# Eight clamps of decoded weight pieces move from VectorE to GpSimd

## The chip, the cores and the metric

The kernel runs on one core of one Trainium2 chip, as one program. The metric is the device time of that core in microseconds. Five engines work side by side, each through its own queue and in the order of that queue: TensorE (PE: matmuls into the accumulator memory PSUM), VectorE (DVE), ScalarE (ACT), GpSimd (POOL) and SyncE (SP: it issues transfers). They meet at semaphores only.

## The reference, cut to what matters

Eight batches of an attention over 32 memory slots per head, whose output goes through a two-layer network with a squared ReLU. q, k, v and phi are float32; the two weight matrices of the network are float64.

```python
a = softmax(phi, over the sequence)          # per memory slot
k_m, v_m = einsum(a, k), einsum(a, v)        # 32 x 64 per head
attn = softmax(q @ k_m.T / 8) @ v_m          # per head
x = attn, laid out as 4608 tokens x 512
h = maximum(x @ w_in, 0)                     # w_in 512 x 2048, float64
out = (h * h @ w_out).astype(float32)        # w_out 2048 x 512, float64
```

## The kernel before

**What is computed where.** TensorE never multiplies `attn` itself: each batch's values are folded into `w_in` first (`u`, by `make_u` or `late_u`), and `u` is multiplied with the attention weights `a` (`ffn1`, L672), squared, and multiplied with `w_out` (`ffn2`, L693 and L701). Batches 0 and 1 run as 64 steps in the order of `runs`; each step is one `ffn1` of 128 rows of `d_ff` and, two steps later, its `ffn2`. In the first 16 steps batch 0 takes an unsplit float32 copy of `u` and `a`; later ones take each factor as a high and a low part. Batches 2 to 7 follow in another scheme (`late_*`), from some 200 us on.

**The weights.** [...] Each matrix is loaded as raw 8-byte words (`fetch_w_in`, `fetch_w_out`) and `decode` turns a piece of 128 x 512 or 128 x 1024 words into float32. There are 17 pieces: `("in", n, q0)` for `w_in`, of which the first two, (0,0) and (0,1), are halves of 128 x 512; `("out", k)` for `w_out`, k from 0 to 7. I write in(0,0) or out 1 for them.

**The steps of one decode, with the lines of the profile:**

1. L575, ScalarE: the upper word of each number, read as float32, loses its sign and goes to the tile `tmp` (two buffers). For in(2,0) VectorE does it instead (L581).
2. L578, ScalarE: the lower word, scaled, goes to the tile `low` (one buffer).
3. L582, VectorE: the magnitude in `tmp` is clamped between `LEAST` and `MOST`, in place: two comparisons in one instruction.
4. L584, VectorE: shift by three bits and mask, in place.
5. L587, VectorE: the sign and the top exponent bit of the upper word are put in; reads the raw piece and `tmp`.
6. L594, the `adder` given by the caller: `tmp` + `low` is the float32 weight. It goes to `w_sb` (for `w_in`) or to `wp` or `tmp` (for `w_out`). It is GpSimd for in(0,0) and in(0,1), VectorE for the other six pieces of the change.

`decode` stops at two places (`yield`), ahead of step 3 and ahead of step 6, and the caller goes on with other work there.

**What sets the order.** It is written out by hand. The string `order` interleaves the first work: `d0`, `d1` and `d2` are the decodes of in(0,0), in(0,1) and in(1,0), `o0` that of out 0, `a0` and `a1` are the two attention halves of batch 0, `v0` and `u0` the two halves of the first `u`. After it, the table `plan` says at which half step each later piece goes on: out 1 at 3, 6 and 8, in(3,0) at 8, 9 and 11, out 2 from 20 on, out 3 from 31 on. Each engine then works off its queue in that order. So L582 of a piece stands at a fixed place between other VectorE instructions, for example between L482 and L584 for in(1,0).

**Other lines that are named below.** L201 and L209 are TensorE's transpose and broadcast for the softmax of `phi` of batch 1 (VectorE's L187 to L190 ahead of them, L204 between them, L223 behind). L434 is `by_heads`, also for the attention scores. In `attend`, VectorE's L460 or L462 transposes the scores, L466 and L470 subtract their maximum, ScalarE's L472 is the exponential, VectorE's L479 to L482 normalise and L487 or L492 transposes back; L494 and L495 (or L502 and L504 in `split_a`) split the result into `a_hi` (ScalarE) and `a_lo` (GpSimd or VectorE). L550 makes `u_lo` on VectorE. L685 makes `g_lo` on GpSimd from step 16 on. L112 fills rows of a tile of keys with zeros, on GpSimd.

Of the kernel before, what the change touches and what calls it, by code (L numbers as in the profile page):

```python
# [14 lines left out]
ALU = mybir.AluOpType  # L15
# [5 lines left out]
LEAST = 2.0 ** -15  # L21
MOST = 2.0 ** 17 - 2.0 ** 13 - 2.0 ** -7
# [3 lines left out]
def attn_moe_kernel(ctx: ExitStack, tc: tile.TileContext, qT, kv, phi, w_in, w_out, outT):  # L26
# [12 lines left out]
    nc = tc.nc  # L39
# [93 lines left out]
    def new_ps(main=False):  # L133

        if starting and not main:
            n = len(starting) - 1
            starting.append(True)
            return [ps_acc.tile([P, 512], F32, name=f"acc{2 * (n % 2) + i}") for i in range(2)]
        assert not ps_user, (now, ps_user)
        ps_user.append(list(now))  # L140
        return ps_m.tile([P, 2, 512], F32, name="ps_m")

    def done_ps(ps):
        if not isinstance(ps, list):
            ps_user.pop()

    def bank(ps, i):
        return ps[i] if isinstance(ps, list) else ps[:, i]
# [279 lines left out]
    def by_heads(out, mem, x, rhs):  # L428

        for pr in range(NPAIR):  # L430
            for half in range(2):
                hs = slice(D * half, D * (half + 1))
                y = rhs[pr // NQ][hs, pr % NQ]
                nc.tensor.matmul(  # L434
                    bank(out, half)[M * pr:M * (pr + 1), :y.shape[-1]], mem[hs, x, pr], y, start=True, stop=True
                )

    def half_heads(out, mem, x, rhs, half):

        hs = slice(D * half, D * (half + 1))  # L440
        for pr in range(NPAIR):
            y = rhs[pr // NQ][hs, pr % NQ]
            nc.tensor.matmul(out[M * pr:M * (pr + 1), :y.shape[-1]], mem[hs, x, pr], y, start=True, stop=True)  # L443
# [117 lines left out]

    on_vector = {("in", 2, 0)}

    def decode(raw, new_out, adder, key):

        n = raw.shape[1] * raw.shape[2]

        def word(w, dtype):
            return raw.bitcast(dtype).rearrange("p j (n w) -> p (j n) w", w=2)[:, :, w]


        c = work.tile([P, 2 * DM], I32, name="tmp", bufs=2)[:, :n]
        size = c.bitcast(F32)
        if key not in on_vector:
            nc.scalar.activation(size, word(1, F32), AF.Abs)  # L575

        r = work.tile([P, 2 * DM], I32, name="low", bufs=1)[:, :n]
        nc.scalar.activation(r, word(0, U32), AF.Copy, scale=2.0 ** -29)  # L578
        yield
        if key in on_vector:  # L580
            nc.vector.tensor_scalar(out=c, in0=word(1, I32), scalar1=0x7FFFFFFF, scalar2=None, op0=ALU.bitwise_and)  # L581
        nc.vector.tensor_scalar(out=size, in0=size, scalar1=LEAST, scalar2=MOST, op0=ALU.max, op1=ALU.min)  # L582

        nc.vector.tensor_scalar(  # L584
            out=c, in0=c, scalar1=3, scalar2=0x3FFFFFF8, op0=ALU.logical_shift_left, op1=ALU.bitwise_and
        )
        nc.vector.scalar_tensor_tensor(  # L587
            out=c, in0=word(1, I32), scalar=-0x40000000, in1=c, op0=ALU.bitwise_and, op1=ALU.bitwise_or
        )
        yield  # L590
        out = c if new_out is None else new_out().bitcast(I32)
        if len(out.shape) > 2:
            c, r = (x.rearrange("p (a n) -> p a n", a=out.shape[1]) for x in (c, r))
        adder.tensor_tensor(out=out, in0=c, in1=r, op=ALU.add)  # L594
        return out.bitcast(F32)
# [19 lines left out]
    def decode_in(n, q0, q1, adder=nc.gpsimd):  # L615

        def new_out():
            if n // 2 not in w_in_at:
                w_in_at[n // 2] = new_w()
            return w_in_at[n // 2][:, 2 * q0:2 * q1, n % 2 * HC:n % 2 * HC + HC]  # L620

        assert all(("in", n, qd) in fetched for qd in range(q0, q1))
        yield from decode(raws["in", n][:, q0:q1], new_out, adder, ("in", n, q0))
        ready.update(("in", n, qd) for qd in range(q0, q1))
        if all(("in", n ^ i, x) in ready for i in range(2) for x in range(NQ)):
            if starting:
                kept.append(n // 2)
                return
            yield
            keep_w(n // 2)  # L630

    def decode_out(k, adder=nc.gpsimd, whole=False):

        def new_out():
            w = room(k, [P, 2, DM], F32)
            wo[2 * k:2 * k + 2] = [w[:, 0], w[:, 1]]
            return w

        assert all(("out", k, i) in fetched for i in range(2))
        w = yield from decode(raws.pop(("out", k)), new_out if whole else None, adder, ("out", k))  # L640
        if not whole:
            yield
            yield from split(k, w.rearrange("p (i x) -> p i x", i=2))
        ready.update(("out", 2 * k + i) for i in range(2))
# [61 lines left out]
    banks = {}  # L706
    current = [-1]

    held = {}

    def hold(name, who):
        assert name not in held, (name, who, held)
        held[name] = who

    def drop(name, who):
        assert held.pop(name) == who
# [227 lines left out]
    def late_u(b, n):  # L944

        assert ("mem", b) in ready
        drop("w", (b, n))
        for i in range(2):
            hold(f"raw{i}", (b, 2 * n + i))
        w = late_rooms["w"]  # L950
        if "raw" not in late_rooms:
            late_rooms["raw"] = work.tile([P, 2, 4, P], F32, name="low", bufs=1)
            late_rooms["e"] = {}
        raw = late_rooms["raw"]
        first = b == JOIN and not n
        x = (state[b]["mem"], 1, [w[:, :NQ], w[:, NQ:]])
        if first:
            ps = new_ps(True)
            by_heads(ps, *x)
        else:  # L960
            assert banks["open"]
            hold("side", ("u", b, n))
            ps = [banks["z" if "m" in held else "m"], banks["h"][(current[0] + 1) % 2]]
            if beside:
                half_heads(*beside.pop(0))
                sc = banks["m"]
                nc.scalar.copy(sc[:, T3:T3 + 1], sc[:, T3 - 1:T3])
                half_heads(ps[1], *x, 1)
                half_heads(ps[0], *x, 0)
                half_heads(*beside.pop(0))  # L970
            else:
                by_heads(ps, *x)
        yield
        for qd in (1, 0):
            (nc.scalar.copy if late_on[f"raw{qd}"] >> n & 1 else nc.vector.tensor_copy)(raw[:, :, 2 * (1 - qd):2 * (1 - qd) + 2], bank(ps, qd).rearrange("p (a i n) -> p a i n", a=2, i=2))
        if first:
            done_ps(ps)
        else:
            drop("side", ("u", b, n))
        ready.update(("raw", b, 2 * n + i) for i in range(2))  # L980

    def late_split(b, p):
# [441 lines left out]
    for places, fn, *args in plan:  # L1424
# [6 lines left out]

    late_plan = [
        ((32, 33), late_u, 0, 3),
        ((0, 1), late_u, 0, 1),
        ((33, 33, 33, 35, 38), late_split, 0, 6),
        ((1, 3, 8, 9, 13), late_split, 0, 2),
        ((18, 19, 21, 22, 24), late_split, 0, 4),
        ((3, 8, 8, 11, 16), late_split, 0, 3),
        ((20,), late_stream, 0, 3),
        ((36, 37, 40, 41, 48), late_split, 0, 7),  # L1440
        ((16, 16), late_u, 0, 2),
        ((7,), late_stream, 0, 2),
        ((21, 22, 27, 27, 32), late_split, 0, 5),
# [92 lines left out]
    for k, step in enumerate(steps):  # L1536
        i, b, t, f = step
# [4 lines left out]
        n = f * P // FC  # L1542
        u, a = state[b]["u"][n][0], state[b]["a32" if alone else "a"][t]
# [50 lines left out]
    z = banks["z"]  # L1594
# [56 lines left out]
    n = (B - JOIN) * REST  # L1651
# [79 lines left out]
```

## Time and profile before

| | us |
|---|---|
| median of three runs | 700.79 (700.62 to 700.91) |
| the profiled execution, first to last instruction (its span) | 698.8 |
| TensorE busy | 683.1 (98%) |
| VectorE busy | 502.3 (72%) |
| ScalarE busy | 437.6 (63%) |
| GpSimd busy | 315.9 (45%) |

The profile shows one execution. Its span runs from the first to the last instruction; the time of a run is taken from outside and holds 1.99 us more (700.79 less 698.8). TensorE's granted clock is 1.00 of full speed, its level of 2.4 GHz, in every stretch of the table of stretches.

Rows of a timeline read: start, duration, engine, line, operation, result <- operands, shape, count, and in brackets the idle time of the engine before it with what ended it. Rows of one engine can overlap by some 0.08 us, because an instruction may start while the last one empties. In the chain of waits each piece begins where the one before it ended; "issue" there is time in which nothing was waited for.

### The profile page before, as it was taken

How to read it: one execution, taken by the hardware profiler on the slowest of the kernel's cores; microseconds unless marked ns; L12 is line 12 of the kernel's file. 1: busy time of each engine (PE TensorE's matmuls, PEld its weight loads, DVE VectorE, ACT ScalarE, POOL GpSimd, SP SyncE). 2: the span in 40 equal slices, each digit the busy share in tenths (PEclk: the TensorE clock that was granted, in tenths of full speed). 3: DMA queues.
4: the chain of work that ended last, by engine and by line, in shares of the span. 5: the costliest groups of instructions: out<-in, count | busy, mean ns of one | idle time of the engine just before them, and what ended most of it. 6: DMA issues, size and time to landing. Idle time of an engine off the chain costs nothing.

```text
span 698.8 us, 14172 instructions
## 1 busy us (share of the span) xinstructions
PE 683.1 (98%) x5104; PEld 574.2 (82%) x5104; DVE 502.3 (72%) x1167; ACT 437.6 (63%) x1204; POOL 315.9 (45%) x481
## 2 busy tenths in 40 slices
PE   8789999999999999999999999999999999999997
PEld 4367889999998888888888887888878888888897
DVE  3988868655888977888878977797787775555432
ACT  2566788886456675567566665667566666665531
POOL 1200253443348465645665564745474566444200
PEclk9999999999999999999999999999999999999999
DMA  9996353509423922184136613291206110400002
GB/s 289 350 376 242 118 175 83 186 2 264 139 62 129 289 75 76 46 244 139 42 121 188 175 61 122 85 275 63 83 1 212 69 51 19 150 32 1 28 33 47
DMA packets 67847, 89.86 MB, mean 129 GB/s; under 512 B 6848, under 2 KB 56064, under 8 KB 64192
## 3 DMA queue, kind: packets, MB, share of 16 engines
q1 hardware_dynamic: 65888, 87.41, 38.7%
q10 hardware_dynamic: 1888, 1.54, 0.7%
q8 instruction: 40, 0.66, 0.4%
q14 instruction: 31, 0.25, 0.1%
HBM read 75.30 MB, written 13.63 MB: 127 GB/s over the span
## 4 chain that ended last, share of the span: by engine, by line
PE 87%; DVE 9%; ACT 1%; issue 1%; POOL 1%; POOLq 0%; DVEq 0%; ACTq 0%
PE acc L1092 35%; PE h L1116 10%; PE acc L701 9%; PE z L1116 7%; PE h L672 6%; PE acc L693 4%; PE h L1681 2%; DVE mem L400 1%; PE ps_m L434 1%; PE z L443 1%; DVE u_lo L996 1%; PE m L1681 1%; PE z L1681 1%; PE m L322 1%; PE m L443 1%; PE h L154 1%
## 5 line engine op out<-in xcount | busy, mean ns | idle before, releaser
L1092 PE MATMUL acc<-u_hi,wp 128*128 128x512 f32 x576 | 153.9, 396 | 0.0
L1092 PE MATMUL acc<-u_lo,wp 128*128 128x512 f32 x576 | 140.0, 392 | 0.0
L1092 PEld LDWEIGHTS acc<-u_hi,wp 128*128 128x128 f32 x576 | 101.2, 188 | 26.0 <-issue 11.0
L1092 PEld LDWEIGHTS acc<-u_lo,wp 128*128 128x128 f32 x576 | 105.5, 188 | 20.4
L996 POOL TENSOR_TENSOR u_lo<-low,u_hi 128x256 fp32r<-128x256 f32 (+1 forms) x106 | 68.9, 661 | 47.8 <-ACT u_hi L995 44.9
L685 POOL TENSOR_TENSOR g_lo<-g,g_hi 128x288 fp32r<-128x288 f32 x48 | 44.4, 925 | 80.6 <-ACT g_hi L683 55.7
L1140 POOL TENSOR_TENSOR u_hi<-g_lo,u_hi 128x288 fp32r<-128x288 f32 (+1 forms) x70 | 53.2, 761 | 43.5 <-ACT g_lo L1137 21.1
L701 PE MATMUL acc<-g_hi,wp 128*128 128x288 f32 x360 | 59.0, 298 | 0.2 <-DVE o L1173 0.2
L995 ACT CAST u_hi<-low 128x256 fp32r<-128x256 f32 (+1 forms) x160 | 52.7, 347 | 8.4 <-POOL low L1007 7.2
L1132 DVE CUSTOM_DVE_ANT_0 g_hi<-h,g_hi 128x288 f32<-128x288 f32 x95 | 42.6, 449 | 19.8 <-ACT g_hi L1163 19.2
L1163 ACT COPY g_hi<-z 128x288 f32<-128x288 f32 x72 | 28.7, 399 | 44.2 <-PE z L1116 43.1
L701 PEld LDWEIGHTS acc<-g_hi,wp 128*128 128x128 f32 x360 | 51.2, 188 | 4.9 <-ACT r L674 1.7
L1135 ACT ACTIVATE u_hi<-g_hi 128x224 fp32r<-128x224 f32 x95 | 39.0, 411 | 22.1 <-DVE g_hi L1132 22.0
L1158 POOL TENSOR_TENSOR u_lo<-g_lo,u_lo 128x288 fp32r<-128x288 f32 x30 | 25.1, 838 | 55.2 <-DVE g_lo L1157 49.2
L674 ACT ACTIVATE r<-h 128x288 f32<-128x288 f32 x64 | 26.0, 406 | 31.6 <-PE h L672 31.5
L1157 DVE TENSOR_TENSOR g_lo<-h,g 128x288 f32<-128x288 f32 x48 | 21.6, 450 | 25.0 <-ACT g L1153 25.0
L693 PE MATMUL acc<-g_hi,wp 128*128 128x288 f32 x128 | 33.8, 410 | 1.6 <-DVE wp L594 1.6
L1116 PE MATMUL z<-a_hi,u_hi 128*128 128x288 f32 x120 | 35.3, 294 | 0.0
L1116 PE MATMUL h<-w_sb,u_hi 128*128 128x288 f32 x120 | 34.3, 298 | 0.8 <-DVE g_hi L1132 0.8
L1116 PE MATMUL h<-a_lo,u_hi 128*128 128x288 f32 x120 | 34.6, 295 | 0.0
L701 PE MATMUL acc<-g_lo,wp 128*128 128x288 f32 x180 | 34.6, 295 | 0.0
L1135 ACT ACTIVATE u_lo<-g 128x224 fp32r<-128x224 f32 x48 | 18.8, 391 | 23.6 <-DVE g L1132 23.5
(366 smaller groups left out, 1789.5 us busy)
## 6 DMA issues: line engine op xcount, KB each, us to landing
w_sb<-w_f SPq DMA_DIRECT2D x24, 1024.0 KB, 5.2
wp<-in_w_in SPq DMA_DIRECT2D x16, 512.0 KB, 8.2
wp<-in_w_out SPq DMA_DIRECT2D x16, 512.0 KB, 7.4
kvb<-in_kv SPq DMA_DIRECT2D x28, 256.0 KB, 7.1
tmp<-in_kv SPq DMA_DIRECT2D x24, 256.0 KB, 6.1
q_sb<-in_q SPq DMA_DIRECT2D x15, 384.0 KB, 5.7
w_f<-w_sb SPq DMA_DIRECT2D x4, 1024.0 KB, 6.2
e_sb<-in_phi SPq DMA_DIRECT2D x7, 512.0 KB, 7.1
```

Source lines behind the costliest of these rows:

```text
L672: nc.tensor.matmul(h[:, :T], u[:, qd, fs], x[:, qd], start=(i == 0), stop=(i == len(todo) - 1))
L685: nc.gpsimd.tensor_tensor(out=g_lo, in0=g, in1=g_hi.bitcast(F32), op=ALU.subtract)
L693: nc.tensor.matmul(acc[e][:, :T], wo[f][:, e * P:(e + 1) * P], g_hi, start=first, stop=last)
L701: nc.tensor.matmul(acc[e][:, :T], wo[f][:, w, e * P:(e + 1) * P], x, start=first and x is g_hi and w == 0, stop=last and x is g_lo,)
L995: nc.scalar.copy(hi[:, k], x)
L996: by(name, p).tensor_tensor(out=lo[:, k], in0=x, in1=hi[:, k].bitcast(F32), op=ALU.subtract)
L1092: nc.tensor.matmul(late_accs[e], wo[f][:, w, e * P:(e + 1) * P], x, start=f == 0 and first, stop=f == NFT - 1 and last,)
L1116: nc.tensor.matmul(out[:, :T], u[:, lhs], a, start=first and not n, stop=n == 2, skip_group_check=not first)
L1132: nc.vector._custom_dve(TENSOR_ADD_SAT, out=x, in0=u[:, :T], in1=x, s0=float("inf"), s1=0.0)
L1135: nc.scalar.square(g_hi, x[:, :n])
L1140: by(f"c{k}", p).tensor_tensor(out=g_lo, in0=g[:, :n], in1=g_hi.bitcast(F32), op=ALU.subtract)
L1163: (nc.vector.tensor_copy if late_on[f"z{k}"] >> pairs[j][1] & 1 else nc.scalar.copy)(x, banks["z"][:, :T])
```

## The change

The diff, whole. `on_pool` names eight pieces, and for these step 3 goes to GpSimd. The second part makes `late_u` record that it holds the bank `m` while it uses it; it chooses the same bank as before.

```diff
     on_vector = {("in", 2, 0)}
 
+    on_pool = {("in", 0, 0), ("in", 0, 1), ("in", 1, 0), ("out", 0), ("out", 1), ("in", 3, 0), ("out", 2), ("out", 3)}
+
     def decode(raw, new_out, adder, key):
...
-        nc.vector.tensor_scalar(out=size, in0=size, scalar1=LEAST, scalar2=MOST, op0=ALU.max, op1=ALU.min)
+        (nc.gpsimd if key in on_pool else nc.vector).tensor_scalar(
+            out=size, in0=size, scalar1=LEAST, scalar2=MOST, op0=ALU.max, op1=ALU.min
+        )
...
-            ps = [banks["z" if "m" in held else "m"], banks["h"][(current[0] + 1) % 2]]
+            own = "m" not in held
+            if own:
+                hold("m", ("u", b, n))
+            ps = [banks["m" if own else "z"], banks["h"][(current[0] + 1) % 2]]
...
             drop("side", ("u", b, n))
+            if own:
+                drop("m", ("u", b, n))
```

In the changed file all lines behind `on_pool` have higher numbers: L582 becomes L584 there, L584 L588, L587 L591, L594 L598, L685 L689.

GpSimd's queue over the whole start, before. In the names, `tmp_253` is in(0,0), `tmp_270` in(0,1), `tmp_308` in(1,0), `tmp_347` out 0, `tmp_438` out 1, `tmp_568` in(3,0), `tmp_753` out 2 and `tmp_896` out 3; `u_hi4_380` is the tile of keys:

```order
L594 TENSOR_TENSOR w_sb_303<-tmp_253,low_255 128x2x256
L594 TENSOR_TENSOR w_sb_303<-tmp_270,low_272 128x2x256
L112 MEMSET u_hi4_380 64x512
L504 TENSOR_TENSOR a_lo0_414<-a_hi2_344,a_hi0_413 128x576
L495 TENSOR_TENSOR a_lo3_771<-at_772,a_hi3_770 128x576
L504 TENSOR_TENSOR a_lo1_640<-u_lo0_436,a_hi1_639 128x576
```

The same stretch of GpSimd's queue now:

```order
L584 TENSOR_SCALAR tmp_253<-tmp_253 128x512
L598 TENSOR_TENSOR w_sb_303<-tmp_253,low_255 128x2x256
L584 TENSOR_SCALAR tmp_270<-tmp_270 128x512
L598 TENSOR_TENSOR w_sb_303<-tmp_270,low_272 128x2x256
L584 TENSOR_SCALAR tmp_308<-tmp_308 128x1024
L584 TENSOR_SCALAR tmp_347<-tmp_347 128x1024
L112 MEMSET u_hi4_380 64x512
L584 TENSOR_SCALAR tmp_438<-tmp_438 128x1024
L584 TENSOR_SCALAR tmp_568<-tmp_568 128x1024
L504 TENSOR_TENSOR a_lo0_414<-a_hi2_344,a_hi0_413 128x576
L584 TENSOR_SCALAR tmp_753<-tmp_753 128x1024
L495 TENSOR_TENSOR a_lo3_771<-at_772,a_hi3_770 128x576
```

The fill of the keys now stands behind the clamps of in(1,0) and out 0, the subtraction of L504 also behind those of out 1 and in(3,0), and that of L495 also behind that of out 2.

VectorE's queue at in(1,0) and out 0, before (`w_sb_303` is the decoded `w_in`, `wp0_406` the decoded out 0):

```order
L482 TENSOR_TENSOR st_277<-st_277,acc1_279 128x576
L582 TENSOR_SCALAR tmp_308<-tmp_308 128x1024
L584 TENSOR_SCALAR tmp_308<-tmp_308 128x1024
L587 SCALAR_TENSOR_TENSOR tmp_308<-wp5_118,tmp_308 128x1024
L487 STREAM_TRANSPOSE a_hi2_344<-st_277 128x576
L594 ISA w_sb_303<-tmp_308,low_310 128x4x512
L582 TENSOR_SCALAR tmp_347<-tmp_347 128x1024
L584 TENSOR_SCALAR tmp_347<-tmp_347 128x1024
L587 SCALAR_TENSOR_TENSOR tmp_347<-wp0_120,tmp_347 128x1024
L594 ISA wp0_406<-tmp_347,low_349 128x2048
```

And now:

```order
L482 TENSOR_TENSOR st_277<-st_277,acc1_279 128x576
L588 TENSOR_SCALAR tmp_308<-tmp_308 128x1024
L591 SCALAR_TENSOR_TENSOR tmp_308<-wp5_118,tmp_308 128x1024
L487 STREAM_TRANSPOSE a_hi2_344<-st_277 128x576
L598 ISA w_sb_303<-tmp_308,low_310 128x4x512
L588 TENSOR_SCALAR tmp_347<-tmp_347 128x1024
L591 SCALAR_TENSOR_TENSOR tmp_347<-wp0_120,tmp_347 128x1024
L598 ISA wp0_406<-tmp_347,low_349 128x2048
```

The two rows of L582 are gone, nothing else has moved, and each L588 now waits for GpSimd.

## Rows read from the trace of the kernel before

**Rows 1.** By stretches: window, length, busy us of each engine, clock, DMA
```profile
46.00:690.00 644.00, 641.81 (x4654) 549.17 (x4654) 468.49 (x1105) 414.03 (x1165) 308.46 (x460) 1.00 0.36 115
```

**Rows 2.** Chain of waits, first 140 us: start us, us, what
```profile
16.52 0.34 DVE tmp L582
...
20.38 0.35 DVE tmp L582
...
23.95 0.70 DVE tmp L582
...
28.42 0.61 DVE tmp L582
...
36.37 0.41 PE ps_m L201 x2
...
39.69 0.46 PE ps_m L209 x4
...
41.72 0.61 DVE tmp L582
```

**Rows 3.** GpSimd by form: count, busy us, mean ns, idle before
```profile
L1001 POOL TENSOR_TENSOR g_hi<-low 128x128 f32<-128x128 f32 x18 | 8.3, 460 | 0.0
...
L594 POOL TENSOR_TENSOR w_sb<-tmp,low 128x1024 int32<-128x1024 int32 x1 | 2.4, 2414 | 0.0
...
L112 POOL MEMSET u_hi<- 64x512 f32 x2 | 1.0, 520 | 0.1
...
masks.py:199 POOL TENSOR_SCALAR_AFFINE_SELECT ident<-ident 128x128 f32<-128x128 f32 x1 | 0.3, 292 | 0.1
```

**Rows 4.** Timeline, 87 to 90 us: start us, us, engine, line, [idle before]
```profile
87.59 1.60 DVE L594 CUSTOM_DVE_ANT_0 tmp<-tmp,low 128x2048 uint16<-128x2048 uint16 x1
...
88.36 1.49 POOL L685 TENSOR_TENSOR g_lo<-g,g_hi 128x288 fp32r<-128x288 f32 x1 [0.25 <-ACT g_hi L683]
...
89.37 1.04 DVE L582 TENSOR_SCALAR tmp<-tmp 128x1024 f32<-128x1024 f32 x1 [0.17 <-ACT tmp L575]
```

**Rows 5.** Timeline of three engines, 69 to 75 us
```profile
69.08 0.76 DVE L482 TENSOR_TENSOR st<-st,sm 128x576 f32<-128x576 f32 x1
...
72.50 2.00 POOL L495 TENSOR_TENSOR a_lo<-at,a_hi 128x576 fp32r<-128x576 f32 x1 [38.85 <-ACT a_hi L494]
...
74.54 0.30 PEld L672 LDWEIGHTS h<-a_lo,u_hi 128*128 128x128 f32 x2 [0.16 <-POOL a_lo L495]
```

**Rows 6.** ScalarE's timeline: absolute values of five pieces
```profile
15.26 0.67 ACT L575 ACTIVATE tmp<-wp 128x512 f32<-128x512 f32 x1 [4.53 <-DMA wp<-in_w_in]
...
22.06 1.15 ACT L575 ACTIVATE tmp<-wp 128x1024 f32<-128x1024 f32 x1 [0.74 <-DMA wp<-in_w_in]
...
26.25 1.19 ACT L575 ACTIVATE tmp<-wp 128x1024 f32<-128x1024 f32 x1
...
35.34 1.12 ACT L575 ACTIVATE tmp<-wp 128x1024 f32<-128x1024 f32 x1
...
67.65 1.14 ACT L575 ACTIVATE tmp<-wp 128x1024 f32<-128x1024 f32 x1
```

**Rows 7.** GpSimd's timeline: the addition of the first piece
```profile
18.22 1.27 POOL L594 TENSOR_TENSOR w_sb<-tmp,low 128x512 int32<-128x512 int32 x1 [14.69 <-DVE tmp L587]
```

**Rows 8.** VectorE's timeline, 27 to 39 us
```profile
27.24 1.18 DVE L594 CUSTOM_DVE_ANT_0 w_sb<-tmp,low 128x2048 uint16<-128x2048 uint16 x1
...
37.44 0.76 DVE L482 TENSOR_TENSOR st<-st,sm 128x576 f32<-128x576 f32 x1
...
38.93 0.39 DVE L204 TENSOR_REDUCE nmx<-ps_m 128x2 f32<-128x256 f32 x1
```

**Rows 9.** TensorE's timeline at 45.7 us
```profile
45.73 2.21 PE L693 MATMUL acc<-g_hi,wp 128*128 128x288 f32 x8 [0.41 <-DVE wp L594]
```

**Rows 10.** VectorE's timeline: two places where its queue stands idle
```profile
52.04 0.78 DVE L462 STREAM_TRANSPOSE st<-ps_m 128x576 f32<-128x576 f32 x1 [1.24 <-PE ps_m L434]
...
95.42 1.22 DVE L550 TENSOR_TENSOR u_lo<-ps_m,u_hi 128x1024 fp32r<-128x1024 f32 x1 [1.89 <-ACT u_hi L548]
```

## The prediction

> **What bounds the kernel now.** I read the busy time of each engine by stretches first: from 46 to 690 us TensorE is busy for nearly all of the 644 us [rows 1]. So whatever happens beside it there is free as long as it is not late. Then I read the chain of waits over the first 140 us, because the eight clamps all stand early. Before TensorE's L201 at 36.37 us, and again between its L209, which ends at 40.15, and 45.7 us, the chain runs mostly on VectorE, and the clamp of L582 is on it five times: 0.34, 0.35, 0.70, 0.61 and 0.61 us [rows 2]. These belong to the pieces in(0,0), in(0,1), in(1,0), out 0 and out 1. The other three moved clamps, in(3,0), out 2 and out 3, are not on the chain. So the most that the change could take off is 2.6 us (the five added up), and only if GpSimd hands each clamped piece over before VectorE would have wanted it.
>
> That the change does not do what it says can be excluded from the order of the instructions: eight clamps leave VectorE and eight stand on GpSimd, and no other row of any engine differs. The `hold` and `drop` lines in `late_u` only record who uses a bank and leave no instruction behind.
>
> **The price of a clamp on GpSimd.** The trace has no such instruction there. GpSimd's two-input additions take 0.46 us for 128 elements a partition and 2.41 us for 1024, so 2.18 ns an element and 0.17 to 0.18 us fixed. The one instruction there that reads one tile and writes one, the mask of 128 elements, takes 0.29 us: with the same fixed part, 0.12 us for 128 elements, or 0.94 ns an element. The fill, which reads nothing, takes 0.52 us for 512 [rows 3]. The clamp reads one tile and writes one, like the mask, so I take the mask's rate: 0.66 us for 512 elements and 1.14 us for 1024. The ends are the fill's rate (0.52 us, and twice its 0.34 above the fixed part, 0.86 us, for 1024) and the two-input rate (1.30 and 2.41 us).
>
> The Trainium skill (GPSIMD Engine Reference, Engine selection) says that one-input work on GpSimd is roughly at line rate and that elementwise work otherwise belongs on VectorE, where it is about twice as fast. By its clock of 1.2 GHz, 1024 elements would be about 0.85 us plus the fixed part, an estimate that would make the sum some 0.2 us smaller than mine.
>
> **One port between the two engines.** At 87.59 us VectorE's addition of L594 (two tiles read) starts and ends at 89.19; GpSimd's subtraction that starts at 88.36 takes 1.49 us and ends 0.66 us after VectorE's end. The next VectorE clamp starts at 89.37, while that subtraction runs, and takes 1.04 us: it ends 0.56 us after GpSimd's end, where an undisturbed one takes 0.70 (at 23.95) [rows 2, 4]. So the one that is second stands until the first is done, and then needs about 0.13 us less than alone.
>
> The Trainium skill (SBUF — State Buffer, Who interferes with whom) says the same: the pair of ports is locked for a whole instruction, against VectorE instructions with two SBUF inputs or in a two-port mode. The trace agrees, with the 1.04 us above.
>
> **The change part by part.** A hand-over between GpSimd and another engine takes 0.04 us where TensorE waits for it (74.50 to 74.54 [rows 5]); I take 0.05 each way.
>
> in(0,0): the absolute value is done at 15.26 + 0.67 = 15.93 us [rows 6]. The clamp runs from 15.98 to 16.64 on GpSimd and L584 starts at 16.69; before, it started at 16.88 (16.52 + 0.34 + 0.02). VectorE itself is free at 16.52. Gain 0.19.
>
> in(0,1): GpSimd must first finish the addition of in(0,0), at 19.49 [rows 7], now 19.30. The clamp ends at 19.96. VectorE reaches this place at 20.38 - 0.19 = 20.19, so nothing waits. Gain 0.19 + 0.37 = 0.56.
>
> in(1,0): the absolute value waited for its weights from memory and ends at 22.06 + 1.15 = 23.21 whatever VectorE does [rows 6]. The clamp runs to 24.40, L584 starts at 24.45, and before at 24.67 (23.95 + 0.70 + 0.02). Of the 0.56 us gained, 0.22 are left: VectorE now waits where it had worked.
>
> out 0: here the port decides. VectorE's addition for in(1,0) started at 27.24 [rows 8] and now starts at 27.02, and it ends at 28.20. The absolute value of out 0 ended at 27.44 (26.25 + 1.19 [rows 6]); it stands on ScalarE behind work that moves with in(0,0), so it ends at 27.25 at best. GpSimd is second, stands until 28.20, needs 1.01 us more, and L584 starts at 29.26. Before, it started at 29.05. So up to here the change loses 0.21 us. From here the chain stays on VectorE until TensorE's L201 at 36.37 us [rows 2], which waits for it, so the loss goes through. GpSimd's fill for the keys is queued behind this clamp and no longer before it; the keys are multiplied only after L209 [rows 2], more than 10 us later, so I cost it at nothing. If it got the port just ahead of L584, that would cost up to its 0.52 us [rows 3].
>
> out 1: the absolute value ends at 36.46 [rows 6], the clamp at 37.65, more than 3 us before VectorE needs it, at 41.72 [rows 2]. It collides with L482, which reads two tiles and starts at 37.44 [rows 8]: 0.21 us, less the 0.13. VectorE's L204 ends at 38.93 + 0.39 = 39.32 and TensorE's L209 starts at 39.69 behind other TensorE work [rows 2, 8], so 0.3 us are hidden there. Then 0.71 us are gone from VectorE ahead of the addition for out 1, whose result TensorE awaited for 0.41 us at 45.73 [rows 9]. Behind that wait comes TensorE's own preceding work. Gain 0.41.
>
> in(3,0) and out 3: the VectorE queue behind them waits anyway, 1.24 us for TensorE at 52.04 and 1.89 us for ScalarE at 95.42 [rows 10]. The subtraction of L504, now queued on GpSimd behind the clamps of out 1 and in(3,0), slips from 32 us to 46 us; its result belongs to a later use of the split, since the first 16 steps take the unsplit copy. Nothing for all of these; if the cover were gone, each would cost one clamp, 1.1 us.
>
> out 2: the clamp starts at 67.65 + 1.14 + 0.05 = 68.84 on GpSimd, 0.24 us before VectorE's L482 at 69.08, which reads two tiles. L482 stands until 69.98 and ends at 70.61 instead of 69.84, 0.77 late; the removed clamp gives back 0.71 (as at 23.95). The subtraction of L495 on GpSimd comes out of this queue, and TensorE waits for it with no slack at 74.54 [rows 5]. Loss 0.06.
>
> **Sum.** 698.8 + 0.21 - 0.41 + 0.06 = 698.7 us of span. The median of the runs, 700.79, is 1.99 us above the profiled span; I add that to every sum here. Forecast 700.7.
>
> **Rivals.** *GpSimd's clamp is slow* (slower). The place is out 0 and then out 2, through the port. At 1.78 us for 1024, halfway to the two-input rate, in(1,0) is 0.42 late, the clamp of out 0 comes in ahead of VectorE's addition (27.62 against 27.66), and that stands until 29.40: L584 is 1.40 late. At out 1, L482 stands for 0.85 us, which eats the gain of 0.41. At out 2 another 0.70 is lost. Together 2.1, so 702.9; at the full two-input rate about 4, so 704.8. Between -0.1 at 1.14 us and 2.1 at 1.78 us, it passes 1.4 us of loss at about 1.58 us. For it speaks that this is two comparisons in one instruction, which no row shows; against it the mask's rate.
>
> *No lock for one-input work* (a little faster). If GpSimd ran beside VectorE, out 0 would be clamped at 28.44 and L584 would gain 0.56 instead of losing 0.21; with the 0.41, 699.8. Against it speaks that the VectorE instruction that stood at 89.37 was a one-input one.
>
> With the fill's rate and the lock, L584 of out 0 gains 0.35, in all some 0.7: 700.1. That is the near end of the forecast, not another case.
>
> **How the numbers follow.** Forecast 0.60, the slow clamp 0.24, no lock 0.11, and 0.05 for something unseen on either side. The measurement tells about 0.2%, 1.4 us, from no change. The forecast and the unlocked case lie within that; the slow clamp lies above it from 1.58 us on, most of its weight. So faster 0.06, same 0.71, slower 0.23. The range goes from 699.7 (no lock) to 703.0 (the slow clamp's 702.9); the full two-input rate and a gain beyond 1.1 us are left out.
>
> **What would show it.** A GpSimd clamp of 1024 elements at 1.0 to 1.3 us where nothing runs beside it; VectorE idle before L588 (the old L584) for in(1,0), about 1 us, with GpSimd as the one that ends it; GpSimd's clamp of out 0 stretched to 2 us across VectorE's addition; no TensorE wait at out 1. I am wrong if that clamp takes 1.6 us or more alone, if out 0 is clamped before 28.2 us, or if TensorE's gap at 74.5 us has grown by more than 0.3 us.

## The result: 708.1 us, ratio 1.0097, and the profile after

The changed kernel takes 708.1 us (median, 706.48 to 709.29) against 700.79 us: a ratio of 1.0097, 95% interval 1.0084 to 1.011. That is slower by some 6.8 us, where the prediction expected 700.7 and allowed up to 703.0. The span of the profiled execution is 705.4 us, against 698.8.

The first view is the line L584 by itself (duration in ns, least/median/most; first and last start; forms). It answers to [rows 3].

```profile
L584 POOL TENSOR_SCALAR tmp<-tmp x8: 1916/3622/4161, 15.7 to 89.1; 128x1024 f32<-128x1024 f32 x6, 128x512 f32<-128x512 f32 x2
...
who waited for it (us, times):
  DVE tmp L588: 12.0, 6
```

A clamp takes 1.92 us for 512 elements and 3.62 for 1024, where VectorE took 0.41 and 0.69. VectorE waited for it six times, 12.0 us in all. The chain of waits (start us, us, what) shows where that lies on the path; it answers to [rows 2], in which the clamp stood five times with 0.34 to 0.70 us and always on VectorE.

```profile
15.73 1.93 POOL tmp L584
...
20.26 1.89 POOL tmp L584
...
24.72 3.63 POOL tmp L584
...
89.13 3.88 POOL tmp L584
...
93.04 1.30 DVE tmp L588
...
97.47 1.17 ACT low L580
```

The pieces in(0,0), in(0,1) and in(1,0) now put GpSimd itself on the chain. So does out 3 at 89.13, which was not on the chain at all before. In VectorE's timeline (start us, us, what, idle before and what ended it) the waits of the start are these:

```profile
17.68 0.43 DVE L588 TENSOR_SCALAR tmp<-tmp 128x512 int32<-128x512 int32 x1 [1.49 <-POOL tmp L584]
...
22.17 0.43 DVE L588 TENSOR_SCALAR tmp<-tmp 128x512 int32<-128x512 int32 x1 [1.00 <-POOL tmp L584]
...
28.37 0.69 DVE L588 TENSOR_SCALAR tmp<-tmp 128x1024 int32<-128x1024 int32 x1 [2.98 <-POOL tmp L584]
29.10 1.94 DVE L591 SCALAR_TENSOR_TENSOR tmp<-wp,tmp 128x1024 int32<-128x1024 int32 x1
...
32.76 0.92 DVE L588 TENSOR_SCALAR tmp<-tmp 128x1024 int32<-128x1024 int32 x1
```

The sum of the start: 1.49 + 1.00 + 2.98 = 5.47 us of waiting; L591 at 29.10 needs 1.94 us instead of 1.23, because GpSimd's clamp of out 0 gets going beside it, 0.71 more; and L588 at 32.76 needs 0.92 instead of 0.69, because GpSimd's fill L112 (32.61, 0.52 us) came in ahead of it, 0.23 more. That makes 6.41. The four clamps that left VectorE gave back 0.41 + 0.42 + 0.69 + 0.68 = 2.20, and this execution reached this place 0.32 us earlier (L412 at 15.78 instead of 16.10). 6.41 - 2.20 - 0.32 = 3.89, and TensorE's L201 is 3.93 us later, at 40.30 instead of 36.37 [rows 2].

TensorE's timeline gives the lateness at six places. First after, then the rows of before that [rows 2, 9] don't hold:

```profile
40.30 0.41 PE L201 MATMUL ps_m<-ident,phi_mx 128*128 128x128 f32 x2
...
49.69 2.21 PE L697 MATMUL acc<-g_hi,wp 128*128 128x288 f32 x8
...
65.40 0.53 PE L676 MATMUL h<-a_hi,u_hi 128*128 128x288 f32 x2 [0.33 <-ACT a_hi L494]
...
79.56 2.10 PE L697 MATMUL acc<-g_hi,wp 128*128 128x288 f32 x8
...
99.93 0.53 PE L676 MATMUL h<-a_hi,u_hi 128*128 128x288 f32 x2 [0.52 <-ACT r L678]
107.88 1.44 PE L705 MATMUL acc<-g_hi,wp 128*128 128x288 f32 x8 [0.74 <-ACT o L1189]
```

```profile
60.73 0.64 PE L672 MATMUL h<-a_hi,u_hi 128*128 128x288 f32 x2
...
74.91 2.10 PE L693 MATMUL acc<-g_hi,wp 128*128 128x288 f32 x8
...
94.60 0.43 PE L672 MATMUL h<-a_hi,u_hi 128*128 128x288 f32 x2
...
101.26 1.33 PE L701 MATMUL acc<-g_hi,wp 128*128 128x288 f32 x8
```

Late by 3.93 at L201; by 3.96 at the weights of out 1 (49.69 against 45.73 [rows 9]), where the old wait is gone but nothing was won on the whole; by 4.67 behind in(3,0) (65.40 against 60.73); by 4.65 behind out 2 (79.56 against 74.91); then by 5.33 (99.93 against 94.60) and 6.62 (107.88 against 101.26), each behind a wait for ScalarE that before did not have. It stays at 6.6 to the end (705.4 less 698.8). So in this execution the first four pieces cost 3.9 us (4.2, if the 0.32 that it was ahead is taken out), out 1 nothing, in(3,0) 0.7, out 2 nothing and out 3 about 2.

### The profile page after: what moved, and what is told of

Same layout as the page of the kernel before. It is cut to its first block, busy times and chain, and to the rows that moved or that the text cites. A ratio compares the mean times of both kernels' runs of the same rounds, so it can differ in the third digit from the quotient of the medians.

```text
span 705.4 us, 14175 instructions
## 1 busy us (share of the span) xinstructions
PE 685.6 (97%) x5104; PEld 575.2 (82%) x5104; DVE 502.7 (71%) x1159; ACT 437.7 (62%) x1204; POOL 340.3 (48%) x489
## 3 DMA queue, kind: packets, MB, share of 16 engines
q10 hardware_dynamic: 1888, 1.54, 0.7%
## 4 chain that ended last, share of the span: by engine, by line
PE 80%; DVE 10%; ACT 4%; POOL 2%; DMA 2%; issue 1%; SPq 0%; POOLq 0%; ACTq 0%; DVEq 0%
PE acc L1101 35%; PE h L1125 10%; PE acc L705 8%; PE z L1125 7%; PE h L676 5%; PE h L1690 2%; PE acc L697 2%; POOL tmp L584 2%; DMA wp<-in_w_in 1%; DVE mem L400 1%; PE z L443 1%; DVE u_lo L1005 1%; PE m L1690 1%; PE z L1690 1%; PE m L322 1%; PE m L443 1%
## 5 line engine op out<-in xcount | busy, mean ns | idle before, releaser
L689 POOL TENSOR_TENSOR g_lo<-g,g_hi 128x288 fp32r<-128x288 f32 x48 | 43.3, 904 | 72.2 <-ACT g_hi L687 40.4
L584 POOL TENSOR_SCALAR tmp<-tmp 128x1024 f32<-128x1024 f32 (+1 forms) x8 | 26.4, 3302 | 52.7 <-ACT tmp L577 52.7
L678 ACT ACTIVATE r<-h 128x288 f32<-128x288 f32 x64 | 26.1, 408 | 30.8 <-PE h L676 30.6
```

What stands on the lines that cost most here:

```text
L584: (nc.gpsimd if key in on_pool else nc.vector).tensor_scalar(out=size, in0=size, scalar1=LEAST, scalar2=MOST, op0=ALU.max, op1=ALU.min)
L689: nc.gpsimd.tensor_tensor(out=g_lo, in0=g, in1=g_hi.bitcast(F32), op=ALU.subtract)
```

## The experiments

**What a clamp costs alone.** Behind the end of the kernel before, GpSimd runs instructions in threes on tiles full of ones, and then beside short VectorE instructions. `clamp(n, op0, op1)` stands for three tensor_scalar instructions on n elements with these one or two operations.

```diff
+    clamp(1024, ALU.max, ALU.min)
+    clamp(512, ALU.max, ALU.min)
+    clamp(1024, ALU.max)
+    clamp(512, ALU.max)
+    clamp(1024, ALU.add)
+    for _ in range(3):
+        nc.gpsimd.tensor_copy(y, x)
+    clamp(1024, ALU.mult, ALU.add)
```

> The kernel before, with GpSimd instructions added behind its end, where nothing else runs: clamps of 1024 and 512 elements with two comparisons, with one, an addition, a multiply-add, a copy, each three times; then clamps beside a train of VectorE instructions that read two tiles (40 of 128 elements), and beside a train of two-port ones (40 of 256). Its time is not read. Price by the kind of instruction: if the two comparisons are the price, one comparison on 1024 elements takes about half of 3.6 us; if it is this kind of instruction on GpSimd, all of them take 3.6 us (1.9 us for 512) and only the copy is near 1 us. Port: if a clamp locks it for its whole duration, a VectorE instruction stands for 3.5 us beside each; if only for its reading, for about 1 us, as L480 and L482 seemed to in the changed kernel.

GpSimd's timeline, one row of each three, in that order (max alone on 512 elements left out):

```profile
695.73 3.63 POOL L1701 TENSOR_SCALAR tmp<-tmp 128x1024 f32<-128x1024 f32 x1
...
705.15 1.92 POOL L1701 TENSOR_SCALAR tmp<-tmp 128x512 f32<-128x512 f32 x1
...
712.01 2.76 POOL L1701 TENSOR_SCALAR tmp<-tmp 128x1024 f32<-128x1024 f32 x1
...
725.26 2.77 POOL L1701 TENSOR_SCALAR tmp<-tmp 128x1024 f32<-128x1024 f32 x1
...
730.94 1.04 POOL L1714 COPY tmp<-tmp 128x1024 f32<-128x1024 f32 x1
...
734.26 1.04 POOL L1701 TENSOR_SCALAR tmp<-tmp 128x1024 f32<-128x1024 f32 x1
```

The 3.62 us of the kernel are the clamp's own price: undisturbed, it takes 3.63. One input and one output do not make it cheap. A copy takes 1.04 us, and so does a multiplication with an addition in one instruction; a lone max takes 2.76, a lone add 2.77, and max with min 3.63. So the price hangs on which operations the instruction carries. Neither expectation held: one comparison takes more than half, and not all tensor_scalar instructions are dear. A multiplication alone was not timed, and why the operations differ stays open.

The last part holds GpSimd's clamp beside a train of VectorE additions of 128 elements (two inputs, 0.29 us each). GpSimd's and VectorE's timelines:

```profile
738.37 3.73 POOL L1701 TENSOR_SCALAR tmp<-tmp 128x1024 f32<-128x1024 f32 x1 [0.81 <-DVE low L1717]
```

```profile
738.65 1.00 DVE L1719 TENSOR_TENSOR low<-tmp 128x128 f32<-128x128 f32 x1
...
739.69 0.29 DVE L1719 TENSOR_TENSOR low<-tmp 128x128 f32<-128x128 f32 x1
...
742.29 1.07 DVE L1719 TENSOR_TENSOR low<-tmp 128x128 f32<-128x128 f32 x1
```

One addition stands for 0.7 us at the clamp's start, and from 739.69 on the train runs at full speed although the clamp goes on to 742.10. The next one to stand is that at 742.29, 0.10 us into the next clamp. The port is not held for the whole clamp: of the two cases expected, it is the second, with 0.7 us instead of about 1.

**One comparison instead of two.** The upper comparison is left out on GpSimd.

```diff
-        (nc.gpsimd if key in on_pool else nc.vector).tensor_scalar(
-            out=size, in0=size, scalar1=LEAST, scalar2=MOST, op0=ALU.max, op1=ALU.min
-        )
+        if key in on_pool:
+            nc.gpsimd.tensor_scalar(out=size, in0=size, scalar1=LEAST, scalar2=None, op0=ALU.max)
...
```

> The changed kernel, with the upper bound of the clamp left out in the eight pieces on GpSimd (one comparison instead of two). If the second comparison is half of the price, a clamp of 1024 takes about 2.0 us, VectorE's waits at the start shrink, and the time is about 702 to 703. If not, 707 as before.

704.89 us, ratio 1.0072 (1.0047 to 1.0096). By form, GpSimd's list reads:

```profile
L585 POOL TENSOR_SCALAR tmp<-tmp 128x1024 f32<-128x1024 f32 x6 | 17.7, 2943 | 41.9 <-ACT tmp L577 33.4 <-DVE phi_mx L190 7.4 <-DMA wp<-in_w_out 1.1
```

The instruction is shorter by 0.8 us (2.94 on average instead of 3.76, port waits included), not by the 1.6 us of the first expectation, and the time lies between the two that were expected. The ratio is lower than that of the changed kernel, 1.0097, but the intervals overlap, so this run alone doesn't show that the loss follows the price; the run at the predicted price does.

**The start alone and the late pieces alone.** Of the eight keys only the first four, or only the last three, stay on GpSimd.

```diff
-    on_pool = {("in", 0, 0), ("in", 0, 1), ("in", 1, 0), ("out", 0), ("out", 1), ("in", 3, 0), ("out", 2), ("out", 3)}
+    on_pool = {("in", 0, 0), ("in", 0, 1), ("in", 1, 0), ("out", 0)}
```

> Only in(0,0), in(0,1), in(1,0) and out 0 on GpSimd. If VectorE's waits for these four are the loss of the start, TensorE's matmuls with out 1 start 4.0 us later than before plus the 0.4 that out 1 had given back, and the time is 704.8 to 705.2. If the late pieces are the main loss, under 703.

```diff
+    on_pool = {("in", 3, 0), ("out", 2), ("out", 3)}
```

> Only in(3,0), out 2 and out 3 on GpSimd. By the trace of the changed kernel these cost 2.6 us behind the 4.0 of the start: 703.3 to 703.5. If that part was a consequence of the late start, under 701.5.

The first four give 705.97 us, ratio 1.0067 (1.0042 to 1.0092), the last three 703.89, ratio 1.0042 (1.0031 to 1.0053). Together 1.0109, beside 1.0097 for all eight: the two losses add up within their intervals, and each was a little larger than expected. Above the medians of before they are 5.3 and 3.2 us, together 8.5, where all eight lose 7.3. The first four alone hold a collision that the whole change does not have: in this run's profiled execution VectorE's L187 takes 1.90 us at 37.88 instead of 0.68, beside GpSimd's L504 at 37.26. In the changed kernel L504 stands behind two more clamps and L187 takes 0.69. These 1.2 us are about what the two parts have too much. Out 1 needs neither a gain nor a loss in this sum.

**The same eight places at the predicted price.** This is the run that tests the sum. The instruction stays where it is, in number, size and order, but it multiplies by 1 and adds 0, which takes 1.04 us instead of 3.63; the prediction had reckoned with 1.14.

```diff
-        (nc.gpsimd if key in on_pool else nc.vector).tensor_scalar(
-            out=size, in0=size, scalar1=LEAST, scalar2=MOST, op0=ALU.max, op1=ALU.min
-        )
+        if key in on_pool:
+            nc.gpsimd.tensor_scalar(
+                out=size, in0=size, scalar1=1.0, scalar2=0.0, op0=ALU.mult, op1=ALU.add
+            )
...
```

> The changed kernel with all eight GpSimd clamps in place, but each is a multiplication by 1 and an addition of 0 in one tensor_scalar instead of max and min, so the clamping itself is left out. Behind the end of the first experiment such an instruction took 1.04 us for 1024 elements, where the clamp took 3.63, and the prediction's price was 1.14. Theory (only the price of a GpSimd clamp was wrong, the rest of the sum holds): instruction about 1.05 us (1024) and 0.6 us (512) where nothing runs beside it, the loss before TensorE's L201 within 0.3 us of nothing, no VectorE wait above 0.5 us at out 3, median 700.3 to 701.2. Rival (a hand-over to GpSimd and back costs of itself, whatever the instruction's price): VectorE still waits for GpSimd at in(3,0) and out 3, ScalarE's queue is held, median 702 or more.

701.34 us beside 701.04 for the kernel before, ratio 1.0001 (0.9992 to 1.001). The rival falls: giving a step to GpSimd and taking it back costs nothing here by itself, as far as some 0.7 us either way can be told. Two parts of the expectation were missed: VectorE waits 0.94 us for GpSimd at out 3, where at most 0.5 was expected, and the start loses 0.34 us instead of at most 0.3. Forecast was 700.7 against 700.79, that is no change, and at the price that it was made for there is none. The rows (GpSimd's timeline, then VectorE's) show how far the single steps hold:

```profile
26.96 1.56 POOL L585 TENSOR_SCALAR tmp<-tmp 128x1024 f32<-128x1024 f32 x1 [3.14 <-PE acc L434]
28.58 0.52 POOL L112 MEMSET u_hi<- 64x512 f32 x1
```

```profile
23.86 0.70 DVE L593 TENSOR_SCALAR tmp<-tmp 128x1024 int32<-128x1024 int32 x1 [0.98 <-POOL tmp L585]
...
28.55 1.09 DVE L593 TENSOR_SCALAR tmp<-tmp 128x1024 int32<-128x1024 int32 x1 [0.95 <-POOL tmp L585]
...
36.82 0.74 DVE L480 TENSOR_TENSOR sm<-sm,eps 128x18 f32<-128x18 f32 x1
```

**out 1 alone.**

```diff
+    on_pool = {("out", 1),}
```

> Only the clamp of out 1 goes to GpSimd. Theory: it runs from 36.5 to about 40.2 us, before VectorE wants it at 41.7, holds VectorE's two-input work for at most 0.8 us at its start (L482 at 37.44 comes about 0.9 us after that, so by 0.1 us or so), and the 0.71 us that leave VectorE end TensorE's wait of 0.41 us at 45.7: median 0.2 to 0.5 us below before, 700.2 to 700.5. Rival (the clamp holds the port for its whole 3.6 us, or delays L482 and L204 so that L209 and L223 are later by more than is won): 700.7 to 702.5.

701.12 us, ratio 0.9999 (0.999 to 1.0008): the expected gain of 0.2 to 0.5 us did not come. VectorE's, then TensorE's timeline (this execution runs 0.81 us later as a whole, L201 at 37.18):

```profile
37.73 0.76 DVE L480 TENSOR_TENSOR sm<-sm,eps 128x18 f32<-128x18 f32 x1
```

```profile
40.77 0.71 PE L209 MATMUL ps_m<-ident,nmx 128*128 128x128 f32 x4 [0.26 <-DVE nmx L204]
...
46.58 2.21 PE L697 MATMUL acc<-g_hi,wp 128*128 128x288 f32 x8
```

TensorE's wait for the weights of out 1 is gone, as foreseen: no bracket stands at 46.58. But the small addition L480, which reads two tiles and takes 0.18 us elsewhere, stands for 0.58 us at the clamp's start. L204 behind it is late, TensorE's L209 waits 0.26 us for it, and all that TensorE does from there to out 1 comes later by about as much as the old wait. This is the second case of the rival, with L480 in the place of L482. From L201 to out 1 it is 9.40 us here and 9.36 before (45.73 - 36.37 [rows 2, 9]).

**out 3 alone and in(3,0) alone.**

```diff
+    on_pool = {("out", 3),}
```

> Only the clamp of out 3 goes to GpSimd. Theory (the cover of 1.89 us in front of VectorE at 95.42 isn't enough for 3.6 us, ScalarE's queue is held behind the weights' low words and TensorE's activations come late): VectorE waits for GpSimd 2.5 to 3.6 us, TensorE waits at two places for ScalarE, median 1.2 to 2.2 us above before, 701.9 to 702.9. Rival (the loss of the three late clamps, 3.2 us, comes from in(3,0) and out 2): within 0.5 us of before, 700.3 to 701.2.

```diff
+    on_pool = {("in", 3, 0),}
```

> Only the clamp of in(3,0) goes to GpSimd. Theory: it runs from 45.2 to 48.9 us, VectorE wants it at 46.9 and waits about 1.9 us, has 0.7 less to do, and of the 1.2 that are left the idle time of 1.24 us before 52.04 covers part only, because the clamp's start also holds VectorE's neighbours: 0.3 to 0.9 us above before. Rival 1 (the cover holds): within 0.2 us. Rival 2 (in(3,0) carries most of the 1.1 us that out 3 leaves of the three late ones): 1.0 to 1.5 us above.

out 3 gives 702.96 us, ratio 1.0026 (1.0017 to 1.0035), in(3,0) 702.29, ratio 1.0019 (1.001 to 1.0027). Above the medians of before that is 1.9 and 1.3 us, together the 3.2 us of the three late pieces (703.89 - 700.7), so out 2 costs nothing that can be seen. Out 3 came as expected. The ScalarE timeline shows how its wait spreads:

```profile
92.45 1.18 ACT L580 ACTIVATE low<-wp 128x1024 int32<-128x1024 uint32 x1 [3.49 <-DVE tmp L598]
```

L580 writes the low words of the next piece into the one buffer that VectorE's addition L598 has yet to read. VectorE is late because it waited 3.51 us for GpSimd ahead of L588 at 88.01, and because two subtractions L689, queued on GpSimd behind the clamp, then hold L588 for 1.30 us instead of 0.69 and L591 for 1.71 instead of 1.23. So ScalarE stands for 3.49 us, and the activations of the product, L678, are queued behind L580 on the same engine. That is what TensorE waits for at 99.93 and 107.88 in the changed kernel. For in(3,0) the theory expected less. VectorE's, GpSimd's and TensorE's rows:

```profile
49.09 1.89 DVE L588 TENSOR_SCALAR tmp<-tmp 128x1024 int32<-128x1024 int32 x1 [2.33 <-POOL tmp L584]
```

```profile
49.03 1.40 POOL L504 TENSOR_TENSOR a_lo<-a_hi,a_hi 128x576 fp32r<-128x576 f32 x1
```

```profile
61.59 0.53 PE L676 MATMUL h<-a_hi,u_hi 128*128 128x288 f32 x2 [0.58 <-ACT a_hi L494]
```

The subtraction L504, which was at 32 us before, is queued behind the clamp and starts with its end. So VectorE, which waited 2.33 us for that clamp, stands another 1.20 us at the port (1.89 instead of 0.69). The idle 1.24 us [rows 10] do not cover 2.33 + 1.20 - 0.69. That is rival 2 of this run, and its reason. The clamp itself took 4.32 us here (44.74 to 49.06), because it started inside VectorE's addition L598; in the changed kernel it started at the end of that addition (49.19) and took 3.68. These 0.6 us are about what lies between the 1.3 us of this run and the 0.7 read from the changed kernel's trace.

**TensorE's clock.** In the changed kernel TensorE stands still for 4.82 us before 32.98, and the granted clock between 30 and 40 us is 0.83 instead of 1.00: for a part of the time it is at its lower level of 1.2 GHz, where before it was at 2.4 all through. Eight matmuls at 33.83 take 3.60 us instead of 2.21. To see whether that carries part of the loss, four groups of matmuls without use fill the gap.

```diff
-         "e e e e e m d0 m m m d1 d0 a0 a0 a0 a0 d0 d1 d2 d1 a0 d2 u0 s a1 u0 a0 d2 o0 v0 o0 v0"
+         "e e e e e m d0 m m m d1 d0 a0 a0 a0 a0 d0 d1 d2 d1 a0 d2 u0 s a1 u0 a0 d2 o0 s s s s v0 o0 v0"
```

> The changed kernel with all eight clamps on GpSimd, and four groups of matmuls without use more in TensorE's 4.8 us gap before 33 us, so that the granted clock has less reason to fall (0.83 between 30 and 40 us in the changed kernel). Theory (the loss of the start runs along VectorE; TensorE's lower clock lies beside it): within 0.5 us of the changed kernel in the same comparison, 706 to 708.5, whatever the clock does. Rival (the lower clock carries a part of the loss, eight matmuls that took 2.2 us took 3.6): the granted clock of 30 to 40 us goes up and the median comes down by 1 us or more, to 705.5 or less.

The clock stays up between 30 and 40 us (by stretches: window, length, busy us of PE, PEld, DVE, ACT, POOL, clock, DMA share and GB/s), first this run, then the changed kernel:

```profile
30.00:35.00 5.00, 5.00 (x30) 2.55 (x29) 3.42 (x4) 2.22 (x4) 3.53 (x2) 1.00 1.12 291
35.00:40.00 5.00, 3.54 (x14) 2.20 (x12) 4.76 (x8) 2.58 (x6) 0.00 (x0) 1.00 1.05 359
```

```profile
30.00:35.00 5.00, 2.02 (x19) 1.10 (x20) 4.90 (x5) 1.67 (x2) 3.07 (x2) 0.83 0.89 240
35.00:40.00 5.00, 5.00 (x19) 3.75 (x17) 4.79 (x8) 3.50 (x7) 0.00 (x0) 0.83 1.04 359
```

And the time does not come down: 708.73 us, ratio 1.0107 (1.0093 to 1.0121), a little above the range expected. The run is not quite clean. In its profiled execution the clock was 0.67 between 20 and 25 us, ahead of the added matmuls; there eight matmuls took 5.40 us instead of 3.70, GpSimd's clamp of out 0 came later behind them, and VectorE waited 1.54 us for it. So a low clock can get onto VectorE's path. But another of the four executions had a mean clock of 1.000 and took 708.30 us, 7.3 above before: the loss is there at the full clock too. And in the changed kernel's own trace L201 starts 0.15 us after VectorE's L190 has ended (40.30 and 40.15), just as before (36.37 and 36.22): there VectorE is the limit, and what TensorE loses to the clock lies beside it. The rival falls; what the clock adds to single executions was not measured.

**Which of the first four.**

```diff
+    on_pool = {("in", 0, 0), ("in", 0, 1)}
```

> Only the clamps of in(0,0) and in(0,1), 512 elements each, go to GpSimd. Theory (the price of 1.92 us each is what VectorE waits for: 1.49 and 1.00 us in the changed kernel, less the 0.34 and 0.35 that leave VectorE, and the chain to TensorE's L201 passes it on): 1.4 to 2.0 us above before. Rival (the wait for in(1,0)'s weights behind them, whose absolute value ends at 23.2 us, takes most of it up): within 0.7 us of before.

```diff
+    on_pool = {("in", 1, 0), ("out", 0)}
```

> Only the clamps of in(1,0) and out 0, 1024 elements each, go to GpSimd. Theory: in(1,0)'s clamp runs from 23.3 to 26.9 us, VectorE waits for it some 2.9 us and has 0.7 less to do; out 0's clamp follows at once, to 30.5, and VectorE needs it at about 30.6, so the second wait is short; with the fill that gets in ahead (0.2 to 0.5) and one stand at the port (up to 0.8) 1.8 to 3.3 us above before. Rival (the two clamps add up, 3.6 us each less the 0.7 that leave VectorE): 5 us or more above before. With the two pieces of the run before, the sum should be that of the four, 4.7.

in(0,0) and in(0,1) cost little: 701.9 us, ratio 1.0011 (1.0001 to 1.002), less than the 1.4 us expected. in(1,0) and out 0 cost 705.57 us, ratio 1.0064 (1.0045 to 1.0083), more than the 3.3 us expected. Neither expectation held, though the two ratios together, 1.0075, agree with the 1.0067 of the four within the intervals. For the pair in(1,0) and out 0 the profiled execution shows what was missing in the reckoning (VectorE, then GpSimd):

```profile
28.21 0.69 DVE L588 TENSOR_SCALAR tmp<-tmp 128x1024 int32<-128x1024 int32 x1 [2.92 <-POOL tmp L584]
...
38.46 1.90 DVE L187 TENSOR_TENSOR at<-e_sb 128x512 f32<-128x512 f32 x1
```

```profile
37.84 1.98 POOL L504 TENSOR_TENSOR a_lo<-a_hi,a_hi 128x576 fp32r<-128x576 f32 x1 [4.80 <-issue]
```

The wait is as long as expected. But L187, which takes 0.68 us in before, stands for 1.2 us at the port beside L504, which the delay had moved there from 32 us; the reckoning had left L504 out. This execution also came 1.2 us late to L482 ahead of all that, with a TensorE wait of 1.1 us for a load of queries. The collision at L187 stands in the profiled execution of the first four too; how often the late start comes was not shown. For in(0,0) and in(0,1) it stays open why the median lost only 0.9 us: the profiled execution was the slowest of the twelve (700.51 to 703.2 us), with waits of 1.38 and 0.98 us, as expected, so it can't tell where the other executions make that good. The first of the two waits is not the same in every execution: in other profiled executions with this clamp on GpSimd it is 1.49 us (the changed kernel), 0.93 (the first four) and 0.52 (the run for the clock), while the second stays at 1.00, 1.00 and 0.99.

No version that beats the kernel before came out of this: at a third of the price the eight clamps gain nothing, and out 1 alone gains nothing.

## Why the prediction was wrong, step by step

**The price of a clamp failed.** The step is the one that took the mask's rate because the clamp, too, reads one tile and writes one. It gave 0.66 and 1.14 us; measured are 1.92 and 3.62, three times as much. Worse, the upper end of its range of prices, 1.30 and 2.41 us, was the rate of GpSimd's dearest instruction with two inputs, as if one input could never cost more than two. Nothing in the trace said so: of its kind [rows 3] held only the mask, and the prediction itself noted that two comparisons in one instruction had no row. Of its three signs of being wrong this is the one that came: the clamp takes more than 1.6 us alone. With the price at 1.04 us the measured ratio is 1.0001 (0.9992 to 1.001), so this one term is the whole error in the result, as far as 0.7 us can be told.

The Trainium skill (GPSIMD Engine Reference, Engine selection) calls one-input work on GpSimd roughly line-rate. The copy and the multiply-add, at 1.04 us for 1024 elements, agree with that; max, add and max with min, at 2.76, 2.77 and 3.63, do not.

**The removed part was right.** Five clamps of VectorE stood on the chain, and they left it.

**in(0,0), in(0,1), in(1,0).** At the price assumed they went as written: in the multiply-add run VectorE waits for none of the first two, and 0.98 us before L593 for in(1,0), where about 1 us was foretold. At the real price it waits 1.49, 1.00 and 2.98 us.

**out 0.** Foretold was a clamp stretched to 2 us across VectorE's addition, and a loss of 0.21. In the multiply-add run it is stretched to 1.56, and GpSimd's fill comes in ahead of VectorE and stretches L593 to 1.09, the case that the prediction had named and priced at up to 0.52. L201 comes at 36.27 there, 0.10 ahead of [rows 2], but that execution was 0.44 ahead already at L412 (15.66 instead of 16.10): from there the start loses 0.34, near the 0.21 foretold with a part of the fill.

**out 1 was wrong, and hidden by the rest.** The gain of 0.41 does not exist. The prediction looked for the collision at L482 and found it small; it falls on L480 at the clamp's start (0.74 and 0.76 us instead of 0.18, in the multiply-add run and in out 1 alone), and the 0.3 us that it reckoned as hidden before L209 do not cover it. Only that TensorE no longer waits for the weights was right.

**in(3,0) and out 3 lost their cover.** The prediction named it, 1.24 and 1.89 us [rows 10], and priced its loss at one clamp each. At 1.04 us it holds: in the multiply-add run VectorE doesn't wait at in(3,0), and at out 3 it waits 0.94 us and has 0.69 less to do, which leaves 1.57 of its 1.89 us of idle time at 95.3. At 3.6 us it does not, and the loss, 1.3 and 1.9 us, is not the excess of the clamp but what hangs on VectorE's lateness: L504 and L689 at the port, and ScalarE's queue behind the low words.

**out 2 was right.** Its loss of 0.06 was to be nothing much, and it stays so even at 3.62 us: TensorE's lateness is 4.67 before and 4.65 behind it. The gap at 74.5 us [rows 5] did not grow, it closed, since GpSimd's L495 ran undisturbed in 1.41 us instead of 2.00. VectorE does come late there, but before it stood idle for 2.99 us ahead of L658 (79.70), which the prediction did not count; 0.21 us of that are left in the changed kernel.

**The slow rival had the sign, not the mechanism.** It sent the loss through the port, at out 0 and out 2, and went up to 704.8 us. The port takes 0.71 us at out 0 and nothing on the path at out 2; the loss is VectorE waiting for the result, of which the rival had only 0.42 us, at in(1,0), because its price was too small for more. Its rule that the second of the two engines stands until the first is done held for the multiply-add (L480 at 36.82 ends with the instruction of 36.49 to 37.53), but not for the real clamp, beside which VectorE stands some 0.7 of 3.6 us.

## What to carry to other kernels

Before a step is moved to another engine, find the price of that very operation on that engine; a row of another operation with the same count of inputs can be off by three, and where no row exists the upper bound must come from what the move would have to cost to hurt, not from the dearest row at hand. Then give each cover its size and ask at which price it is gone: here 1.2 and 1.9 us of idle time were enough for 1.04 us and too small for 3.62. A step that lies off the path may still hold a buffer of one, and then the queue behind that buffer is late with it.

## What the runs showed of the hardware

A GpSimd tensor_scalar on 1024 fp32 elements takes 1.04 us with multiply and add, 2.76 with max alone, 2.77 with add alone, 3.63 with max and min: two operations can be cheaper than one of them.

VectorE's two-input instructions stand only for about 0.7 us at the start of such a clamp, not for its 3.6 us. The Trainium skill (SBUF — State Buffer, Who interferes with whom) has the pair of ports held for the whole instruction; the trains of the first experiment show otherwise for this instruction. In the second train, of tensor_scalar instructions with one input (0.29 us each), VectorE stands twice within one clamp (754.47 to 758.29):

```profile
754.75 1.01 DVE L1723 TENSOR_SCALAR low<-tmp 128x256 f32<-128x256 f32 x1
...
757.43 1.00 DVE L1723 TENSOR_SCALAR low<-tmp 128x256 f32<-128x256 f32 x1
758.47 1.08 DVE L1723 TENSOR_SCALAR low<-tmp 128x256 f32<-128x256 f32 x1
```

The first is at the clamp's start, the second 3 us later, near its end, and the third at the start of the next clamp. The additions of the first train, with two inputs, stand at the start only: one at 741.97, across the end of a clamp, takes 0.29 us. One reading is that the clamp fetches its input in one go at the start and writes its output in one go at the end; that is argued from these rows, not shown.
